# Second layer of a routed two-layer network: TensorE's order written out by pairs of slots, and up products that stream a high weight plane and its low partner in 512 columns

## The chip, the cores and the metric

The kernel runs on one core of a Trainium2 chip. A core has five engines, each with its own instruction stream, which meet at semaphores: TensorE (PE in the profile, its weight loads PEld), VectorE (DVE), ScalarE (ACT), GpSimd (POOL) and SyncE (SP), which only issues DMAs here. All time is device time in microseconds; the metric is the time of one execution. Three runs of the kernel before took 458.08, 459.53 and 459.67 us, a median of 459.53 us.

## The reference

The input goes through three parts. The first is an mLSTM over 768 steps for 2 x 8 heads of 40 columns. The second is a dense layer of 1536 tokens by 320 columns, with 2048 hidden columns and a softplus. The third is the second layer, and only it is touched by the change:

```
logits = x @ w_gate                       # 1536 tokens, 8 experts
e_idx  = argmax(logits)                   # one expert per token
gate_w = softmax(logits)[e_idx];  eom = sigmoid(x @ w_output_gate)
for e in range(8):                        # w1[e]: 320 x 1024, w2[e]: 1024 x 320
    h  = relu(x[e_idx == e] @ w1[e])
    out[e_idx == e] = gate_w * eom[:, e] * (h @ w2[e])
```

## The kernel before, in words

**Slots.** The tokens have been scattered into rows ordered by expert, and a slot is 128 such rows of one expert; NS = 15 slots are computed (four more that the code provides for have no work in the profiled execution). Each slot needs an up product (its 128 x 320 rows by the 320 x 1024 of w1), a relu, and a down product (128 x 1024 by the 1024 x 320 of w2), scaled per token by `cc`.

**Rounds.** The 1024 hidden columns are taken in NQ = 4 rounds (`qn`) of FQ = 256. In a round every slot has one up product into PSUM (`ph`), its relu, two transposes of 128 x 128 on TensorE (`tp`), and one down product of DM = 320 columns (`yp`), which is added to the slot's row of `yac`. The last round stores each `yac` row with an indirect DMA on POOL as soon as it is complete.

**Two-part operands.** Matmul operands are fp32r, so each fp32 number is split into a high part and a low part. `w1s` has five planes for each expert: three of high parts (rows 0 to 127, 128 to 255, and 256 to 319 with their low parts below them), then the low parts of the first two. `x2h` and `x2l` hold a slot's rows, turned, in high and low parts; `hh_` (printed as flat, as is `x2h`) and `hl_` (hl) the hidden columns. An up product is eight matmuls of 256 columns (`passes`, line 816), a down product six of 320. The weights are split anew in every round: a raw tile comes by DMA into a ring of seven buffers, ACT casts the high part (`split_w1`, line 1195; `split_w2`, line 1220), DVE subtracts for the low part (`low_w1`, line 1208; `low_w2`, line 1248), and POOL for the half plane of w1 (`low_w1p`, line 1214). Splits of w1 for the next round wait for this round's last up (`w1_read`), those of w2 for its last down (`w2_read`).

**What sets the order.** The instructions are emitted by a planner, the class `Weaver` (line 45). A task is a Python generator; each `yield` names the engines that its next step may run on ("A" ACT, "V" DVE, "G" POOL, "P" PE, "S" SP), a list of events to wait for, or takes a buffer from a `Ring`. The planner keeps a clock of each engine with prices of its own (`Priced`, line 149) and always emits the step that could start first; its rank decides a tie. Of several engines it takes the one that could start first, with a handicap of 10 us on DVE unless it is named first (`LAST`, line 42). Each engine then runs its instructions in the order emitted. In the second layer PE is asked for by several tasks: `slots` (line 1334) turns the rows of a slot, `up2` (line 1384) multiplies, `post` (line 1362) does relu, transposes and split, and `down2` (line 1417) begins a round's downs when its ups are done, in the last round as soon as it can. PSUM has eight banks: two for `ph`, three shared by the turned rows and `tp`, three for `yp`.

Nearly all instructions are emitted through one helper, so that the profile shows line 195 for them; the tile names tell them apart.

Of the kernel before, what the change touches and what calls it, by code (L numbers as in the profile page):

```python
# [23 lines left out]
P = 128  # L24
# [209 lines left out]
def mlstm_moe_kernel(ctx: ExitStack, tc: tile.TileContext, q_t, k_t, k, v, i_gate, f_gate, o_gate,  # L234
# [973 lines left out]
    def low_w1(qn, r, dst, ev):  # L1208
        yield "V"
        vsub(dst[:, 3:5], r[:, 0:2], dst[:, 0:2].bitcast(F32))  # L1210
        W.signal(ev)
        W.signal(w1_ready[qn])
# [35 lines left out]
    def low_w2(qn, e, r, ev):  # L1248
        yield "V"
        vsub(right["w2s"][:, 1, :, e, :], r, right["w2s"][:, 0, :, e, :].bitcast(F32))  # L1250
        W.signal(ev)
        W.signal(w2_ready[qn])
# [61 lines left out]
    ring = {t: Ring(ps2, t, n) for t, n in (("h", 2), ("t", 3), ("y", 3))}  # L1314
    ring["x"] = ring["t"]
# [12 lines left out]
    hr_ring = Ring(lp, "hr", 3)  # L1328
# [5 lines left out]
    def slots():  # L1334
        for s in range(NS):
            yield [slot_row[s]]
            row, row_ev = srow.pop(s)
            if s > 1:
                yield [begun[s - 2]]
            xp, ev = yield from ring["x"].get([P, 3, P], F32, "xslot")  # L1340
            yield "P"
            for kk in range(3):
                PE.transpose(xp[:, kk, :], row[:, kk * P:(kk + 1) * P], ident)
            W.signal(row_ev)
            W.add(after(W.cur.out, slot_x(s, xp, ev)), 0.1)
            W.add(after(slot_row[s], slot_c(s, row, row_ev)), 3)
# [15 lines left out]
    def post(qn, s, ph, hev):  # L1362
        hr, hr_ev = yield from hr_ring.get([P, FQ], F32, "hr")
        yield "AV"
        if W.cur.on == "A":
            ACT.activation(out=hr, in_=ph, func=AF.Relu)
        else:
            DVE.tensor_scalar(out=hr, in0=ph, scalar1=0.0, scalar2=None, op0=ALU.max)
        W.signal(hev)
        tp, ev = yield from ring["t"].get([P, 2, P], F32, "tp2")  # L1370
# [3 lines left out]
        W.signal(hr_ev)  # L1374
        if qn:
            yield [h_read[qn - 1, s]]
        yield "AV"
        copy(hh_[:, s], tp)
        yield "V"
        vsub(hl_[:, s], tp, hh_[:, s].bitcast(F32))  # L1380
# [3 lines left out]
    def up2():  # L1384
        for qn in range(NQ):
            yield [w1_ready[qn]]
            for s in range(NS):
                if qn == 0:
                    yield [slot_ready[s]]
                ph, hev = yield from ring["h"].get([P, FQ], F32, "ph2")  # L1390
                for n, (wt, xt, st, sp) in enumerate(passes(lambda a: w1v[:, a, bass.ds(evals[s] * FQ, FQ)], x2h[:, s], x2l[:, s])):
                    if n % 4 == 0:
                        yield "P"
                    PE.matmul(ph, xt, wt, start=st, stop=sp)
                if qn == 0:
                    W.signal(begun[s])
                W.add(after(W.cur.out, post(qn, s, ph, hev)), 1)
            W.signal(w1_read[qn])

    def reduce2(qn, s, yp, ev):  # L1400
        yield "V"
        if qn == 0:
# [14 lines left out]
    def down2():  # L1417
        for qn in range(NQ):
            yield [w2_ready[qn]] + ([w1_read[qn]] if qn < NQ - 1 else [])
            for s in range(NS):  # L1420
                yield [h_ready[qn, s]]
                yp, yev = yield from ring["y"].get([P, DM], F32, "yp")
                ew = bass.ds(evals[s] * DM, DM)
                order = [(j, xx, wi) for j in range(2) for xx, wi in ((hh_, 0), (hh_, 1), (hl_, 0))]
                for n, (j, xx, wi) in enumerate(order):
                    if n % 3 == 0:
                        yield "P"
# [132 lines left out]
```

## Time and profile before

| | |
|---|---|
| median of three runs | 459.53 us (458.08 to 459.67) |
| the profiled execution: its own time, its span | 458.13 us, 456.4 us |
| PE busy over the span | 421.3 us, 92% |
| DVE, ACT, POOL busy | 332.5, 309.3, 133.1 us (73%, 68%, 29%) |
| mean granted clock of TensorE | 0.965 of 2.4 GHz |
| from the first turned row of the second layer to its last PE product | 303.2 to 451.0 us |

The span runs from the first to the last instruction of the program; the execution's own time has 1.7 us around it. A matmul's recorded duration (some 0.3 us) is longer than the distance to the next one, since they are pipelined; the cost of one in a run of them is the distance between their starts.

In the rows below, a stage is printed as from:to and its length, then the busy time of PE, PEld, DVE, ACT and POOL with the number of instructions in brackets, then the granted clock of TensorE as a share of 2.4 GHz, the DMA engines' share and GB/s. A row of an engine in order of time has start, length, engine, line, operation, out<-in, the shapes and the count of instructions merged; a bracket behind it has the idle time before it and what ended it. A group has its count, its busy time, the mean of one in nanoseconds, and the idle time before its instructions with what ended it. `xslot` is the PSUM tile of turned rows.

### The profile page before, as it was taken

Reading aid. Unit: us, or ns where it says so; the run is one execution under the profiler, and the core shown is the slowest. Engines: PE = TensorE matmul, PEld = TensorE weight load, DVE = VectorE, ACT = ScalarE, POOL = GpSimd, SP = SyncE. Lnnn points to the kernel's source line nnn. Section 1 sums busy time; section 2 is a strip of 40 time slices with the busy share of each in tenths; the row PEclk is TensorE's granted clock in tenths of the full one; section 3 lists DMA queues with packets and bytes.
Section 4 is the critical chain, followed back from the end, with each engine's and each line's share of the span. In section 5 each row is a group of like instructions: output and inputs, shape, how many; then the busy total and the mean of one; then the engine's idle time right before and its main releaser. Section 6 shows DMA issues by size and latency. Waiting matters only on the chain.

```text
span 456.4 us, 10188 instructions
## 1 busy us (share of the span) xinstructions
PE 421.3 (92%) x3189; PEld 402.4 (88%) x3189; DVE 332.5 (73%) x866; ACT 309.3 (68%) x881; POOL 133.1 (29%) x222
## 2 busy tenths in 40 slices
PE   8669999999979999999999999768999999999694
PEld 7558999999879999999999998448899999999683
DVE  2998988769999998856666676565489499498332
ACT  1569799997769997887786786526656557638030
POOL 5256665545123410101010110231060060050633
PEclk9886999999999999999999999879999999999987
DMA  8969739396349423000010000175338348262211
GB/s 268 320 205 285 246 102 299 128 331 182 119 154 338 127 93 87 1 2 4 32 37 2 35 37 2 44 257 198 95 109 286 126 142 283 85 179 90 74 55 49
DMA packets 31772, 62.91 MB, mean 138 GB/s; under 512 B 3706, under 2 KB 16253, under 8 KB 31718
## 3 DMA queue, kind: packets, MB, share of 16 engines
q1 hardware_dynamic: 30230, 57.87, 39.8%
q0 software_dynamic: 1488, 4.35, 2.6%
q8 instruction: 30, 0.49, 0.4%
q14 instruction: 24, 0.20, 0.1%
HBM read 54.05 MB, written 8.65 MB: 137 GB/s over the span
## 4 chain that ended last, share of the span: by engine, by line
PE 71%; DVE 11%; ACT 11%; issue 4%; DMA 2%; SPq 1%; POOL 0%; POOLq 0%; DVEq 0%; ACTq 0%
PE ph L195 28%; PE acc L195 15%; PE yp L195 10%; ACT ab L195 4%; PE pv L195 4%; PE sp L195 4%; PE tp L195 3%; DVE wta L195 3%; DMA wra<-in_w_in_dram 2%; PE lg L195 2%; ACT w1s L195 1%; PE kv L195 1%; PE qc L195 1%; ACT gh L195 1%; ACT w2s L195 1%
## 5 line engine op out<-in xcount | busy, mean ns | idle before, releaser
L195 ACT ACTIVATE ab<-ab 128x256 f32<-128x256 f32 x192 | 78.2, 418 | 2.7
L195 DVE SCALAR_TENSOR_TENSOR g<-ph,ab 128x256 f32<-128x256 f32 x96 | 40.1, 419 | 24.4 <-ACT ab L195 23.7
L195 PE MATMUL ph<-w1s,flat 128*128 x300 | 56.6, 306 | 0.6 <-DVE w1s L195 0.6
L195 PE MATMUL acc<-win,gh 128*128 128x320 f32 x240 | 56.1, 318 | 0.5 <-ACT gh L195 0.5
L195 PE MATMUL yp<-w2s,flat 128*128 x240 | 54.2, 314 | 0.5 <-ACT flat L195 0.5
L195 POOL TENSOR_TENSOR w1s<-w1raw,w1s 64x256 fp32r<-64x256 f32 x32 | 29.7, 954 | 84.8 <-ACT w1s L195 83.0
L195 DVE TENSOR_TENSOR gl<-g,gh 128x256 fp32r<-128x256 f32 x96 | 46.4, 490 | 8.1 <-ACT gh L195 7.1
L195 ACT ACTIVATE ab<-ph 128x256 f32<-128x256 f32 x96 | 36.3, 379 | 18.1 <-PE ph L195 17.7
L195 ACT ACTIVATE hr<-ph 128x256 f32<-128x256 f32 x60 | 23.1, 385 | 34.2 <-PE ph L195 19.8
L195 PEld LDWEIGHTS ph<-w1s,flat 128*128 128x128 f32 x300 | 43.8, 190 | 1.3 <-DVE w1s L195 0.8
L195 PE MATMUL ph<-win 128*128 128x256 f32 x250 | 42.7, 291 | 0.0
L195 ACT CAST gh<-g 128x256 fp32r<-128x256 f32 x96 | 38.3, 401 | 5.8 <-DVE g L195 5.1
L195 DVE TENSOR_TENSOR hl<-tp,flat 128x256 fp32r<-128x256 f32 x60 | 25.1, 420 | 22.6 <-ACT flat L195 22.5
L195 PEld LDWEIGHTS yp<-w2s,flat 128*128 128x128 f32 x240 | 40.1, 190 | 0.7 <-ACT flat L195 0.7
L195 POOL DMA_INDIRECT rows<-row,rsm x12 | 12.2, 1020 | 94.6 <-ACT ab L195 30.7
L195 PEld LDWEIGHTS acc<-win,gh 128*128 128x128 f32 x240 | 38.6, 189 | 1.0 <-ACT gh L195 1.0
L195 PE MATMUL acc<-win,gl 128*128 128x320 f32 x120 | 37.4, 311 | 0.2 <-DVE gl L195 0.2
L195 PE MATMUL yp<-w2s,hl 128*128 x120 | 37.4, 312 | 0.0
L195 ACT CAST w2s<-w2raw 128x640 fp32r<-128x640 f32 x32 | 22.4, 726 | 21.3 <-PE yp L195 14.3
L195 PEld LDWEIGHTS ph<-win 128*128 128x128 f32 x250 | 35.6, 195 | 0.1
L195 PE MATMUL ph<-w1s,x2l 128*128 x180 | 33.9, 296 | 0.0
L195 PE MATMUL acc<-wou,gh 128*128 128x320 f32 x144 | 32.8, 313 | 0.3 <-ACT gh L195 0.3
(191 smaller groups left out, 1082.3 us busy)
## 6 DMA issues: line engine op xcount, KB each, us to landing
w1raw<-in_w_dram SPq DMA_DIRECT2D x32, 384.0 KB, 3.6
wra<-in_w_in_dram SPq DMA_DIRECT2D x16, 704.0 KB, 9.3
w2raw<-in_w_dram SPq DMA_DIRECT2D x32, 320.0 KB, 3.5
abc<-abc_dram SPq DMA_DIRECT2D x4, 1024.0 KB, 7.8
rows<-pad SPq DMA_DIRECT2D x19, 194.0 KB, 4.3
qT<-in_q_t_dram SPq DMA_DIRECT2D x6, 512.0 KB, 4.0
kn<-in_k_dram SPq DMA_DIRECT2D x5, 416.0 KB, 6.7
vn<-in_v_dram SPq DMA_DIRECT2D x6, 320.0 KB, 6.0
```

The source lines that it names most:

```text
L195: return fn(*args, **kw)
```

## The change

**Order of PE.** One task, `second`, replaces `slots`, `up2` and `down2`, and the transposes leave `post`: all PE work of the second layer is emitted in one written order, while ACT, DVE, POOL and SP are still planned. Four slots' rows are turned first. A round then goes by pairs of slots: two ups, the transposes of the pair before, and in the first round the rows of the pair two ahead. Behind the round's last up come two downs, the remaining transposes, and the other downs. In the last round downs begin behind the eighth up, up to three at a time.

**Up product.** `ph` grows from 256 to 512 columns, a whole bank. The first two matmuls stream a high plane of w1 and its low partner side by side (planes 0 and 3, then 1 and 4), 512 columns each; four more of 256 columns add to the first half: six matmuls in place of eight. ACT copies the second half out, DVE adds the first (`halves_sum`), and the relu moves behind the transposes (`split_h`).

**Rings and engines.** `ph` has three banks, `tp` two (a round's last slot takes one of `ph`), the turned rows share the three of `yp`; `hr` has four buffers. In rounds two to four the low parts of w1 and w2 may also run on POOL ("VG"), and in the first round the scaling of a down product may also run on ACT.

```diff
...
     def low_w1(qn, r, dst, ev):
-        yield "V"
-        vsub(dst[:, 3:5], r[:, 0:2], dst[:, 0:2].bitcast(F32))
+        yield "VG" if qn else "V"
+        (psub if W.cur.on == "G" else vsub)(dst[:, 3:5], r[:, 0:2], dst[:, 0:2].bitcast(F32))
         W.signal(ev)
         W.signal(w1_ready[qn])
 
...
     def low_w2(qn, e, r, ev):
-        yield "V"
-        vsub(right["w2s"][:, 1, :, e, :], r, right["w2s"][:, 0, :, e, :].bitcast(F32))
+        yield "VG" if qn else "V"
+        (psub if W.cur.on == "G" else vsub)(right["w2s"][:, 1, :, e, :], r, right["w2s"][:, 0, :, e, :].bitcast(F32))
         W.signal(ev)
         W.signal(w2_ready[qn])
 
...
     ps2 = tc.tile_pool(name="ps2", bufs=1, space=PSUM, reuse_waits="tile")
     ps2_cm, ps2 = ps2, ps2.__enter__()
-    ring = {t: Ring(ps2, t, n) for t, n in (("h", 2), ("t", 3), ("y", 3))}
-    ring["x"] = ring["t"]
+    ring = {t: Ring(ps2, t, n) for t, n in (("h", 3), ("t", 2), ("y", 3))}
+    ring["x"] = ring["y"]
 
...
-    hr_ring = Ring(lp, "hr", 3)
+    hr_ring = Ring(lp, "hr", 4)
 
-    def slots():
...
+    def turn_row(s):
+        yield [slot_row[s]]
+        row, row_ev = srow.pop(s)
+        xp, ev = yield from ring["x"].get([P, 3, P], F32, "xslot")
+        yield "P"
+        for kk in range(3):
+            PE.transpose(xp[:, kk, :], row[:, kk * P:(kk + 1) * P], ident)
+        W.signal(row_ev)
+        W.add(after(W.cur.out, slot_x(s, xp, ev)), 0.1)
+        W.add(after(slot_row[s], slot_c(s, row, row_ev)), 3)
 
     def slot_x(s, xp, ev):
         yield "AV"
...
-    def post(qn, s, ph, hev):
-        hr, hr_ev = yield from hr_ring.get([P, FQ], F32, "hr")
-        yield "AV"
-        if W.cur.on == "A":
-            ACT.activation(out=hr, in_=ph, func=AF.Relu)
-        else:
-            DVE.tensor_scalar(out=hr, in0=ph, scalar1=0.0, scalar2=None, op0=ALU.max)
+    hr_t, have_hr = {}, {(qn, s): Event() for qn in range(NQ) for s in range(NS)}
+
+    def halves_sum(qn, s, ph, hev):
+        hr_t[qn, s] = hr, _ = yield from hr_ring.get([P, FQ], F32, "hr")
+        yield "A"
+        ACT.copy(out=hr, in_=ph[:, 1])
+        yield "V"
+        DVE.tensor_tensor(out=hr, in0=ph[:, 0], in1=hr, op=ALU.add)
         W.signal(hev)
-        tp, ev = yield from ring["t"].get([P, 2, P], F32, "tp2")
+        W.signal(have_hr[qn, s])
+
+    def turn_h(qn, s):
+        yield [have_hr[qn, s]]
+        hr, hr_ev = hr_t.pop((qn, s))
+        tp, ev = yield from ring["h" if s == NS - 1 else "t"].get([P, 2, P], F32, "tp2")
         yield "P"
         for j in range(2):
             PE.transpose(tp[:, j, :], hr[:, j * P:(j + 1) * P], ident)
         W.signal(hr_ev)
+        W.add(after(W.cur.out, split_h(qn, s, tp, ev)), 1)
+
+    def split_h(qn, s, tp, ev):
         if qn:
             yield [h_read[qn - 1, s]]
         yield "AV"
-        copy(hh_[:, s], tp)
-        yield "V"
-        vsub(hl_[:, s], tp, hh_[:, s].bitcast(F32))
+        if W.cur.on == "A":
+            ACT.activation(out=hh_[:, s], in_=tp, func=AF.Relu)
+        else:
+            DVE.tensor_scalar(out=hh_[:, s], in0=tp, scalar1=0.0, scalar2=None, op0=ALU.max)
+        yield "V"
+        DVE.scalar_tensor_tensor(out=hl_[:, s], in0=tp, scalar=0.0, in1=hh_[:, s].bitcast(F32), op0=ALU.max,
+                                 op1=ALU.subtract)
         W.signal(ev)
         W.signal(h_ready[qn, s])
 
-    def up2():
+    def up(qn, s):
+        yield [slot_ready[s]]
+        ph, hev = yield from ring["h"].get([P, 2, FQ], F32, "ph2")
+        ew = bass.ds(evals[s] * FQ, FQ)
+        both = [(x2h[:, s, i], slice(i, i + 4, 3), slice(0, 2)) for i in range(2)]
+        one = [(xx[:, s, i], i, 0) for xx, i in ((x2h, 2), (x2l, 0), (x2l, 1), (x2l, 2))]
+        yield "P"
+        for n, (xt, a, to) in enumerate(both + one):
+            PE.matmul(ph[:, to], xt, w1v[:, a, ew], start=n == 0, stop=n == 5)
+        if qn == 0:
+            W.signal(begun[s])
+        W.add(after(W.cur.out, halves_sum(qn, s, ph, hev)), 1)
+
+    def down(qn, s):
+        yield [w2_ready[qn], h_ready[qn, s]]
+        yp, yev = yield from ring["y"].get([P, DM], F32, "yp")
+        ew = bass.ds(evals[s] * DM, DM)
+        order = [(j, xx, wi) for j in range(2) for xx, wi in ((hh_, 0), (hh_, 1), (hl_, 0))]
+        yield "P"
+        for n, (j, xx, wi) in enumerate(order):
+            PE.matmul(yp, xx[:, s, j, :], w2v[:, wi, j, ew], start=n == 0, stop=n == 5)
+        W.signal(h_read[qn, s])
+        W.add(after(W.cur.out, reduce2(qn, s, yp, yev)), 2)
+
+    def second():
+        for s in range(min(4, NS)):
+            yield from turn_row(s)
         for qn in range(NQ):
             yield [w1_ready[qn]]
-            for s in range(NS):
+            turned, downed = 0, 0
+            for s0 in range(0, NS, 2):
+                s1 = min(s0 + 2, NS)
+                for s in range(s0, s1):
+                    yield from up(qn, s)
+                if s1 == NS:
+                    W.signal(w1_read[qn])
+                if qn == NQ - 1 and s0 >= 6:
+                    for s in range(downed, min(s0 - 2, downed + 3)):
+                        yield from down(qn, s)
+                        downed = s + 1
+                elif s1 == NS:
+                    for s in range(2):
+                        yield from down(qn, s)
+                    downed = 2
+                for s in range(turned, s0):
+                    yield from turn_h(qn, s)
+                turned = s0
                 if qn == 0:
-                    yield [slot_ready[s]]
-                ph, hev = yield from ring["h"].get([P, FQ], F32, "ph2")
-                for n, (wt, xt, st, sp) in enumerate(passes(lambda a: w1v[:, a, bass.ds(evals[s] * FQ, FQ)], x2h[:, s], x2l[:, s])):
-                    if n % 4 == 0:
-                        yield "P"
-                    PE.matmul(ph, xt, wt, start=st, stop=sp)
-                if qn == 0:
-                    W.signal(begun[s])
-                W.add(after(W.cur.out, post(qn, s, ph, hev)), 1)
-            W.signal(w1_read[qn])
+                    for s in range(s0 + 4, min(s0 + 6, NS)):
+                        yield from turn_row(s)
+            for s in range(turned, NS):
+                yield from turn_h(qn, s)
+            for s in range(downed, NS):
+                yield from down(qn, s)
+            W.signal(w2_read[qn])
 
     def reduce2(qn, s, yp, ev):
-        yield "V"
-        if qn == 0:
+        yield "AV" if qn == 0 else "V"
+        if W.cur.on == "A":
+            ACT.activation(out=yac[:, s], in_=yp, func=AF.Copy, scale=cc[:, s:s + 1])
+        elif qn == 0:
             DVE.tensor_scalar(out=yac[:, s], in0=yp, scalar1=cc[:, s:s + 1], scalar2=None, op0=ALU.mult)
         else:
             DVE.scalar_tensor_tensor(out=yac[:, s], in0=yp, scalar=cc[:, s:s + 1], in1=yac[:, s],
...
-    def down2():
...
     W.add(load_rest(), 0)
     for qn in range(1, NQ):
         W.add(split_w2(qn), 4)
         W.add(split_w1(qn), 3)
-    W.add(up2(), 9.0)
-    W.add(down2(), 8)
+    W.add(second(), 0)
     W.run()
```

## Rows read from the trace of the kernel before

**Rows 1.** Busy time by stage in the second layer (from:to, length, then engines).
```profile
303.20:331.10 27.90, 26.04 (x193) 24.16 (x194) 13.74 (x29) 16.45 (x43) 3.52 (x28) 0.97 0.55 190
331.10:345.60 14.50, 13.96 (x96) 13.56 (x94) 13.30 (x25) 7.43 (x12) 6.90 (x8) 1.00 0.49 147
345.60:364.70 19.10, 19.07 (x148) 18.66 (x148) 11.87 (x22) 13.73 (x36) 0.00 (x0) 1.00 0.60 197
364.70:378.40 13.70, 13.62 (x94) 13.36 (x93) 12.66 (x24) 6.55 (x11) 7.52 (x8) 1.00 0.52 151
378.40:410.90 32.50, 32.41 (x243) 31.79 (x242) 24.95 (x47) 20.75 (x46) 7.52 (x8) 1.00 0.57 179
410.90:451.00 40.10, 34.26 (x241) 32.53 (x240) 20.63 (x39) 15.15 (x38) 13.80 (x14) 0.96 0.21 72
429.80:434.20 4.40, 0.04 (x1) 0.00 (x0) 0.55 (x1) 0.38 (x1) 3.00 (x4) 1.00 0.17 59
434.20:437.90 3.70, 3.61 (x16) 3.32 (x17) 0.85 (x2) 1.40 (x4) 0.00 (x0) 0.54 0.10 38
451.00:456.40 5.40, 0.00 (x0) 0.00 (x0) 0.55 (x1) 0.00 (x0) 0.98 (x1) 0.54 0.08 24
```

**Rows 2.** PE in order of time at the start of the third round.
```profile
378.42 0.75 PE L195 MATMUL ph<-w1s,flat 128*128 x5
...
379.36 0.76 PE L195 MATMUL ph<-w1s,flat 128*128 x5
...
380.51 0.86 PE L195 MATMUL ph<-w1s,flat 128*128 x5
...
381.60 0.38 PE L195 MATMUL tp<-ident,hr 128*128 128x128 f32 x2
381.74 0.84 PE L195 MATMUL ph<-w1s,flat 128*128 x5
```

**Rows 3.** The chain that ended last, three of its pieces (start, length, what).
```profile
398.25 12.77 PE yp L195 x87
...
429.84 4.37 issue
...
451.02 0.56 DVE yac L195
```

**Rows 4.** PE in order of time: the warm-up products ahead of the second layer.
```profile
300.45 2.72 PE L195 MATMUL warm<-ones 128*128 128x512 bf16 x6 [3.85 <-DVE w2s L195]
```

**Rows 5.** Busy time and granted clock of the stretch around those warm-up products.
```profile
300.40:303.20 2.80, 2.72 (x6) 0.69 (x5) 2.51 (x4) 0.00 (x0) 1.50 (x4) 0.50 0.86 249
```

**Rows 6.** PE in order of time in the first round, one pair of slots.
```profile
315.91 0.49 PE L195 MATMUL xslot<-ident,yac 128*128 128x128 f32 x3
316.24 0.38 PE L195 MATMUL tp<-ident,hr 128*128 128x128 f32 x2
...
317.66 0.41 PE L195 MATMUL tp<-ident,hr 128*128 128x128 f32 x2 [0.24 <-ACT hr L195]
```

**Rows 7.** DVE in order of time: the eighth sum of the last round.
```profile
432.27 0.55 DVE L195 SCALAR_TENSOR_TENSOR yac<-yp,cc,yac 128x320 f32<-128x320 f32 x1 [3.74 <-remote]
```

**Rows 8.** Groups of instructions by line and shape, 300 us to the end.
```profile
L195 DVE TENSOR_TENSOR hl<-tp,flat 128x256 fp32r<-128x256 f32 x60 | 25.1, 420 | 22.6 <-ACT flat L195 22.5
...
L195 DVE SCALAR_TENSOR_TENSOR yac<-yp,cc,yac 128x320 f32<-128x320 f32 x45 | 23.8, 544 | 10.8 <-PE yp L195 6.8 <-remote 3.7
L195 DVE TENSOR_TENSOR w2s<-w2raw,w2s 128x640 fp32r<-128x640 f32 x29 | 23.3, 820 | 3.7 <-ACT w2s L195 3.1
L195 ACT ACTIVATE hr<-ph 128x256 f32<-128x256 f32 x60 | 23.1, 385 | 34.2 <-PE ph L195 19.8 <-remote 12.0 <-PE tp L195 2.2
...
L195 POOL TENSOR_TENSOR w1s<-w1raw,w1s 64x256 fp32r<-64x256 f32 x24 | 21.9, 949 | 73.7 <-ACT w1s L195 73.7
L195 DVE TENSOR_TENSOR w1s<-w1raw,w1s 128x512 fp32r<-128x512 f32 x24 | 18.8, 782 | 1.9 <-ACT w1s L195 1.9
```

**Rows 9.** POOL in order of time: one of the stores of the result.
```profile
448.75 0.98 POOL L195 DMA_INDIRECT out_dram<-yac,tki  x1 [0.31 <-issue]
```

More of the change, by code (lines that the diff above doesn't have):

```diff
@@ L1332, in mlstm_moe_kernel @@
     h_read = {(qn, s): Event() for qn in range(NQ) for s in range(NS)}
-    def slots():
-        for s in range(NS):
[L1336 to L1340, printed above, removed]
-            yield "P"
[L1342 to L1346, printed above, removed]
+    def turn_row(s):
[8 more added lines that the diff above has]
+        W.add(after(slot_row[s], slot_c(s, row, row_ev)), 3)
     def slot_x(s, xp, ev):
@@ L1385, in up2 @@
+    def second():
+        for s in range(min(4, NS)):
+            yield from turn_row(s)
         for qn in range(NQ):
             yield [w1_ready[qn]]
-            for s in range(NS):
-                if qn == 0:
-                    yield [slot_ready[s]]
-                ph, hev = yield from ring["h"].get([P, FQ], F32, "ph2")
-                for n, (wt, xt, st, sp) in enumerate(passes(lambda a: w1v[:, a, bass.ds(evals[s] * FQ, FQ)], x2h[:, s], x2l[:, s])):
-                    if n % 4 == 0:
-                        yield "P"
-                    PE.matmul(ph, xt, wt, start=st, stop=sp)
-                if qn == 0:
-                    W.signal(begun[s])
-                W.add(after(W.cur.out, post(qn, s, ph, hev)), 1)
@@ L1415, in reduce2 @@
             tc.add_to_no_dep_group("result", r.ins)
-    def down2():
[L1418 to L1427, printed above, removed]
-                    PE.matmul(yp, xx[:, s, j, :], w2v[:, wi, j, ew], start=n == 0, stop=n == 5)
-                W.signal(h_read[qn, s])
-                W.add(after(W.cur.out, reduce2(qn, s, yp, yev)), 2)
-            W.signal(w2_read[qn])
-    W.add(slots(), 0)
     W.add(load_rest(), 0)
```

## The prediction

> **What bounds the kernel now.** I read the busy time by stage first, because the page's means cover layers that the change leaves alone. From 303.2 us on, the second layer runs as four rounds, one per quarter of the hidden columns: fifteen up products, then fifteen down products. In the first ups, the first downs, the second ups, the second downs and the third round PE is busy 26.04 of 27.9 us, 13.96 of 14.5, 19.07 of 19.1, 13.62 of 13.7 and 32.41 of 32.5 [rows 1]. There PE's own stream sets the end. DVE is close behind in the downs (13.30 of 14.5, 12.66 of 13.7). Only the last round is loose: PE 34.26 of 40.1 us, with 4.4 us in which it does almost nothing, 3.7 us at a mean granted clock of 0.54 behind them, and 5.4 us after its last product.
>
> The second view is PE's order of time, to see whether that stream can be shortened [rows 2]. Right behind a run of downs, one slot's eight up products of 256 columns take 0.94 us (378.42 to 379.36): 0.1175 us each. Two slots later, among the transposes, the eight take 1.09 us (380.51 to 381.60), and up plus transposes 1.23 us (380.51 to 381.74), with no idle named. So in the steady run ups cost about 0.136 us an instruction, more than their columns need.
>
> The third view is the chain that ended last: 87 down products in 12.77 us, 0.147 us each or 0.88 us a slot; the 4.37 us gap, named "issue"; DVE's last sum at 451.02 [rows 3].
>
> **The change part by part.** Nothing before 303.2 us changes, and the two kinds of split that may now run on POOL are those of rounds two to four.
>
> *Up products.* Eight instructions become six: two of 512 columns, four of 256; the columns stay 2048. The trace has no 512-column product of this type. 256 columns take 0.1175 us and 320 take 0.147, so 0.46 ns a column, which makes 512 columns 0.235: nothing gained. The other side is the 512-column bf16 warm-up, six in 2.72 us [rows 4] at a granted clock of 0.50 [rows 5], 0.453 each, 0.227 at full clock. One up then costs 2 x 0.227 to 0.235 + 4 x 0.1175 = 0.92 to 0.94. If 0.136 per instruction were the limit, six would need only 0.82, so the columns set it: I take 0.93, nearer to the rows of this type. The upper bound is that 1.09 stays.
>
> The Trainium skill (TensorE: Matmul & The Clock Gate, Back-to-back issue gap) gives a warm product its columns at full clock plus about 2.5 ns. By that, two joined products save 2.5 ns, 0.3 us over 120 of them, and widening as such is worth nothing. The row disagrees on the size (0.1175 us, where the rule gives 0.109 for 256 columns).
>
> *Turns.* A slot's two transposes lie between 1.23 - 0.94 = 0.29 and two of the 0.11 us below: I take 0.25. Three row transposes take 0.33 us (315.91 to 316.24) [rows 6]: 0.34 with their handover.
>
> *First round.* The transposes now wait: 0.24 us for ACT in the row shown [rows 6], and 27.9 - 26.04 = 1.9 us over the stage. In the written order a slot's rows are turned two pairs before its up, and its transposes come one pair behind, so these waits go. New ups: four rows turned first (12 x 0.11 = 1.3, and 0.6 allowed for rows that land late), 15 x 0.93 = 13.95, eleven more rows 3.74, twelve turns 3.0, and 1.0 allowed for handovers: 23.6 for 27.9, **-4.3 us**. New downs: 15 x 0.88 + 3 x 0.25 + 0.5 allowed at the boundary = 14.45 for 14.5, **0**.
>
> *Second and third round.* Ups 13.95 + 3.0 + 0.5 allowed = 17.45 for 19.1; downs 14.45 for 13.7. Together 31.9 for 32.8, **-0.9**, and for the third 31.9 for 32.5, **-0.6**.
>
> *Last round.* PE has 13.95 + 3.75 + 13.2 = 30.9 us of work. The first downs stand behind the eighth up, some 8.5 us into the round, while all eight w2 pieces are split by then only if ACT and DVE keep their pace: the round before interleaves them with the slots at about one a slot. I allow 2.0 us, between 0 and 4. What is queued behind that wait on PE is everything, but ACT and DVE catch up meanwhile. 32.9 for 40.1: **-7.2**. This takes the 4.4 us gap as gone. With the order of before it fell where two ups and a run of downs had been issued and DVE's eighth sum began only at 432.27, its releaser "remote" [rows 7]; no view shows what held it.
>
> *Added work off PE.* Each slot gets a copy of half a bank on ACT, in place of the relu there (0.385 us, the same shape [rows 8]), the relu moves into the copy behind the transposes, and DVE gets one sum of 256 more: sixty of about 0.42 us, the price of its low halves (hl), 6.3 us a round. In the second ups DVE has 11.87 us busy [rows 1]; 11.87 + 6.3 = 18.2 is more than the 17.45 expected. Starts of such rows overlap a little, and POOL may take some of the w2 low halves (0.82 each on DVE), so it is just hidden. What is late if not: the sum before a pair's transposes, and PE behind it. In the first round the yac products may go to ACT, which is busy only 7.43 of 14.5 us in the downs. In the other downs DVE keeps fifteen yac of 0.544 = 8.2 us, eight w1 low halves at 0.782 = 6.3 and a few sums; POOL takes the surplus. POOL's 64x256 piece takes 0.949 us, so 640 elements some 2.4 us and 512 some 1.9 (estimates in proportion; the lower bound is DVE's 0.82 and 0.78).
>
> Beside POOL, DVE's 512-element halves take 0.782 us, where 0.820 for 640 elements, made beside an idle POOL, would give 0.66: each is lengthened by 0.13. The Trainium skill (SBUF — State Buffer, Who interferes with whom) says that a DVE instruction with two SBUF inputs and a GpSimd one that reads SBUF block each other for the whole instruction, not in part. The trace shows less than that.
>
> *Tail.* The last down leaves one product, one DVE sum and one store as before. POOL's stores follow each other every 0.98 + 0.31 = 1.29 us [rows 9], the last three downs every 0.88: the last store starts about 1 us later. **+1.0**, between 0 and 2.
>
> **Sum.** -4.3 + 0 - 0.9 - 0.6 - 7.2 + 1.0 = -12.0 us. The profiled execution took 458.13 us for its span of 456.4, so 446.1; the median of the runs shown is 459.53, 1.4 above it, so about **447 us**. The allowances in it are 6.5 us: without them 441.
>
> **The rivals.**
> - *The gap stays* (0.18). Its cause is not shown, and stores and PE work overlap again. It costs 4.4 us and, at a clock of 0.54, some 1.7 of the 3.7 us behind it: 447.5 + 6 = 453.5. Against it: the order around it is new, and three earlier rounds with the same instructions have none.
> - *POOL's low halves come late* (0.12). Four w1 halves on POOL and its own eight pieces: 4 x 1.9 + 8 x 0.949 = 15.2 us against downs of 14. If DVE is also held for a whole POOL instruction, each of three boundaries waits about 2 us and the last round's first down 1.5 more: 447.5 + 7.5 = 455. For it: DVE's w1 halves stretched beside POOL. Against: there are only eight per round to share, and DVE may keep most.
> - *Ups stay at 1.09* (0.06): the extra is not per instruction, 60 x 0.16 = 9.6 us, 457.
> - *Slower: PE's fixed order waits for the sums* (0.14). A pair's transposes need ACT's copy (0.385), DVE's sum (0.42) and three handovers, some 1.3 us, of 2.6 us until PE arrives. If a w2 half (0.82) and two hl (0.84) stand in front on DVE, and a cast on ACT, it is about 0.7 us late, and a fixed order has nothing else to issue. In some 25 pairs (seven with row turns, eighteen beside w2 splits): 17.5 us, 465. It decides from 12.0 / 25 = 0.48 us a pair. For it: DVE's 18.2 us above. Against: each engine's sum is still at or under the phase, and the ring of up banks grows to three.
>
> **How the numbers follow.** Forecast 0.50, its own range 441 to 452. The others as given. 0.5% (2.3 us, 457.2 to 461.8) is about what a measurement can tell from no change. Faster by more: 0.50 + 0.18 + most of the 0.12 + half of the 0.06, 0.80. Within: 0.08. Slower: 0.12. The range 440 to 459 takes in all but the slower case.
>
> **What would show it.** Right: first ups near 24 us, a slot's up near 0.93 and up plus turn near 1.18, ACT and DVE with no PE wait behind them, the last round near 33 us without a gap, and a clock that stays at its upper level of 2.4 GHz until the last product. Wrong: a wait of PE's transposes for DVE's sum that returns in every pair; a wait at a boundary for POOL's w1s; a 512-column product well over 0.235 us apart.

## The result, and the profile after

On the chip of the first timing the changed kernel took 448.19 us (447.45 to 448.96, four runs) where the kernel before took 459.07 (458.08 to 459.67, four runs): a ratio of 0.9759 [0.9731, 0.9787]. The forecast was 447.

A second chip gave another picture. There the kernel before took 451.64 us (450.50 to 453.49, ten runs) and the changed one 447.08 (445.69 to 448.39, six runs): 0.9900 [0.9875, 0.9925]. The changed kernel differs by 1.1 us between them, the kernel before by 7.4. The last four experiments ran on a chip where the kernel before took 458.51; it is called the third here, but the record does not tell whether it is the first one again. So every ratio below is to the kernel before on the same chip. A few executions that took far longer than the others of their kernel, the profiled one of the experiment with late downs among them, are left out of every time and row.

The stages of the profiled execution on the first chip (447.45 us, span 445.8), cut where those of [rows 1] were: first ups, first downs, second ups, second downs, third ups, third downs, last round, tail.

```profile
304.00:326.70 22.70, 22.33 (x159) 20.55 (x160) 17.42 (x42) 15.10 (x42) 3.52 (x28) 0.99 0.68 238
326.70:341.00 14.30, 14.30 (x99) 13.93 (x98) 6.69 (x13) 13.16 (x26) 10.22 (x9) 1.00 0.58 171
341.00:358.40 17.40, 17.23 (x115) 15.32 (x115) 13.35 (x30) 13.51 (x35) 7.31 (x4) 1.00 0.59 194
358.40:372.90 14.50, 14.50 (x99) 13.95 (x97) 13.16 (x25) 7.26 (x12) 11.37 (x11) 1.00 0.50 152
372.90:390.70 17.80, 17.03 (x117) 15.54 (x116) 13.61 (x30) 13.19 (x34) 9.44 (x5) 1.00 0.61 204
390.70:405.20 14.50, 14.47 (x99) 13.94 (x97) 13.18 (x24) 7.26 (x12) 11.38 (x11) 1.00 0.51 159
405.20:438.50 33.30, 31.63 (x211) 29.24 (x210) 22.92 (x48) 14.89 (x38) 22.13 (x18) 1.00 0.21 72
438.50:445.80 7.30, 0.02 (x1) 0.00 (x0) 0.95 (x2) 0.00 (x0) 2.08 (x3) 0.68 0.15 53
```

TensorE is busy nearly the whole of every ups and downs stage, and its granted clock is 0.99 of 2.4 GHz in the first ups and 1.00 from there to the last product. The last round has no hole: 33.3 us where it had 40.1. The tail grew from 5.4 to 7.3. The kernel before, profiled on the second chip, has these first ups and this last round:

```profile
303.00:331.10 28.10, 26.08 (x194) 24.16 (x194) 14.12 (x30) 16.58 (x43) 4.20 (x30) 0.96 0.56 196
...
410.60:444.10 33.50, 32.47 (x242) 31.24 (x240) 20.80 (x39) 15.11 (x38) 13.80 (x14) 1.00 0.25 87
```

Its first ups are as slow as on the first chip, but its last round takes 33.5 us: there is no gap to remove. Its chain of waits passes the place of the gap [rows 3] with nothing between products and transposes:

```profile
421.24 7.04 PE yp L195 x48
428.28 1.41 PE ph L195 x12
429.69 0.22 PE tp L195 x2
```

All stages in us, from the same views (the second chip's changed kernel was cut likewise):

| stage | predicted | after, chip 1 | before, chip 2 | after, chip 2 |
|---|---|---|---|---|
| first ups | 23.6 | 22.7 | 28.1 | 22.8 |
| first downs | 14.45 | 14.3 | 13.6 | 14.3 |
| second round | 31.9 | 31.9 | 33.5 | 32.0 |
| third round | 31.9 | 32.3 | 32.4 | 32.3 |
| last round | 32.9 | 33.3 | 33.5 | 33.3 |
| tail | 6.4 | 7.3 | 5.4 | 7.1 |
| sum | 141.15 | 141.8 | 146.5 | 141.8 |

The steady run of the third ups, which answers to [rows 2]:

```profile
378.05 0.83 PE L195 MATMUL ph<-w1s,flat 128*128 x3
378.72 0.52 PE L195 MATMUL ph<-w1s,x2l 128*128 x3
379.07 0.74 PE L195 MATMUL ph<-w1s,flat 128*128 x3
...
380.01 0.60 PE L195 MATMUL tp<-ident,hr 128*128 128x128 f32 x4
380.37 0.82 PE L195 MATMUL ph<-w1s,flat 128*128 x3
```

A pair of slots, two ups and four transposes, goes from 378.05 to 380.37: 2.32 us, 1.16 a slot where it was 1.23. The up right behind transposes takes 1.02 us, the second one 0.94, the four transposes 0.36. All waits of TensorE in the second layer (engine, tile and line, what it waited for, us in total, times, longest):

```profile
PE ph L195 <- DVE hr L195: 1.5, 2, 0.8
PE yp L195 <- POOL w2s L195: 0.8, 1, 0.8
PE xslot L195 <- DMA yac<-rows: 0.2, 1, 0.2
```

The two for DVE's sum fall at the starts of the third and the last round (376.65 and 408.90), where the fourth up needs the bank that the first slot's sum frees; the one for POOL's low half at the last round's first down (415.72). The groups of the second layer that answer to [rows 8]:

```profile
L195 POOL TENSOR_TENSOR w2s<-w2raw,w2s 128x640 fp32r<-128x640 f32 x14 | 26.2, 1892 | 8.9 <-issue 4.9 <-ACT w2s L195 4.0
L195 DVE TENSOR_TENSOR hr<-ph,hr 128x256 f32<-128x256 f32 x60 | 24.6, 421 | 18.6 <-ACT hr L195 15.7 <-issue 2.7
L195 DVE TENSOR_TENSOR w1s<-w1raw,w1s 128x512 fp32r<-128x512 f32 x17 | 15.0, 881 | 4.8 <-ACT w1s L195 4.8
L195 DVE TENSOR_TENSOR w2s<-w2raw,w2s 128x640 fp32r<-128x640 f32 x12 | 14.5, 1207 | 1.9 <-ACT w2s L195 1.9
L195 POOL TENSOR_TENSOR w1s<-w1raw,w1s 128x512 fp32r<-128x512 f32 x7 | 9.7, 1385 | 34.8 <-ACT w1s L195 34.5
```

POOL took 14 low halves of w2 at 1.89 us and 7 of w1 at 1.39. DVE's own low half of w2 beside them rose from 0.82 to a mean of 1.21.

### The profile page after: what moved, and what is told of

Same layout as the page of the kernel before. It is cut to its first block, busy times and chain, and to the rows that moved or that the text cites. A ratio compares the mean times of both kernels' runs of the same rounds, so it can differ in the third digit from the quotient of the medians.

```text
span 445.8 us, 9825 instructions
## 1 busy us (share of the span) xinstructions
PE 415.6 (93%) x3069; PEld 393.1 (88%) x3069; DVE 335.0 (75%) x890; ACT 313.7 (70%) x896; POOL 170.0 (38%) x243
## 4 chain that ended last, share of the span: by engine, by line
PE 71%; ACT 10%; DVE 10%; issue 3%; DMA 3%; POOL 2%; SPq 1%; POOLq 0%; DVEq 0%; ACTq 0%
PE ph L195 25%; PE acc L195 15%; PE yp L195 11%; PE pv L195 5%; ACT ab L195 4%; PE sp L195 4%; PE tp L195 2%; DVE wta L195 2%; DVE w2s L195 2%; DMA wra<-in_w_in_dram 2%; PE kv L195 2%; PE qc L195 2%; PE lg L195 2%; ACT w2s L195 2%; ACT w1s L195 1%
## 5 line engine op out<-in xcount | busy, mean ns | idle before, releaser
L195 DVE SCALAR_TENSOR_TENSOR g<-ph,ab 128x256 f32<-128x256 f32 x96 | 40.1, 419 | 24.9 <-ACT ab L195 24.1
L195 POOL TENSOR_TENSOR w1s<-w1raw,w1s 64x256 fp32r<-64x256 f32 (+1 forms) x39 | 40.8, 1061 | 47.0 <-ACT w1s L195 44.4
L195 ACT ACTIVATE ab<-ph 128x256 f32<-128x256 f32 x96 | 36.3, 378 | 17.8 <-PE ph L195 17.4
L195 PE MATMUL ph<-w1s,flat 128*128 x180 | 47.2, 370 | 1.5 <-DVE hr L195 1.5
L195 DVE TENSOR_TENSOR hr<-ph,hr 128x256 f32<-128x256 f32 x60 | 24.6, 421 | 18.6 <-ACT hr L195 15.7
L195 ACT COPY hr<-ph 128x256 f32<-128x256 f32 x60 | 22.6, 377 | 20.3 <-PE ph L195 19.7
L195 PEld LDWEIGHTS ph<-w1s,flat 128*128 128x128 f32 x180 | 29.7, 189 | 4.5 <-DVE hr L195 1.9
L195 PE MATMUL ph<-w1s,x2l 128*128 x180 | 31.1, 281 | 0.0
```

The source lines that it names most:

```text
L195: return fn(*args, **kw)
```

## The experiments

The first eight ran on the second chip, the last four on the third. The expectations of the first four (eight products to late downs) count from the first chip's 459.1 and 448.2 us, those of the last four from the second chip's 451.6 and 447.1, so it is the differences that can be held against the results.

**Eight products in the written order.**

```
-        both = [(x2h[:, s, i], slice(i, i + 4, 3), slice(0, 2)) for i in range(2)]
+        both = [(x2h[:, s, i], i + 3, 1) for i in range(2)] + [(x2h[:, s, i], i, 0) for i in range(2)]
...
-            PE.matmul(ph[:, to], xt, w1v[:, a, ew], start=n == 0, stop=n == 5)
+            PE.matmul(ph[:, to], xt, w1v[:, a, ew], start=n in (0, 2), stop=n in (1, 7))
```

> The changed kernel with each 512-column up product taken apart again into two of 256: eight instructions a slot, the same columns, the same written order of TensorE, the same copy on ScalarE and sum on VectorE. Theory of the prediction (columns alone set an up's price): a slot still 0.93 us, the time unchanged at 448.2 (within 0.9). Rival (an up product whose address comes from a register also costs a fixed step of some 0.136 us an instruction, as in the steady run before, and the downs and transposes give only part of it back): an up of 1.0 to 1.09 us where ups follow each other, 45 to 60 slots by 0.05 to 0.15, so 450.5 to 457.

449.16 us, ratio 0.9938 [0.9910, 0.9965], against 0.9900 [0.9875, 0.9925] for the changed kernel: about 2 us slower by the medians, between the two expectations, though the two intervals overlap a little. TensorE at the start of its second ups shows both of them in turn:

```profile
341.13 0.75 PE L195 MATMUL ph<-w1s,flat 128*128 x5
...
342.07 0.82 PE L195 MATMUL ph<-w1s,flat 128*128 x5
...
343.15 0.82 PE L195 MATMUL ph<-w1s,flat 128*128 x5
...
344.24 0.82 PE L195 MATMUL ph<-w1s,flat 128*128 x5
...
345.33 0.60 PE L195 MATMUL tp<-ident,hr 128*128 128x128 f32 x4
```

The first up takes 0.94 us, the next three 1.08 to 1.09: 0.136 an instruction, the pace of the steady run before [rows 2]. With six products the four ups in this place take 0.93 to 0.95 each (340.97 to 344.73 on the first chip). Later, with four transposes behind every pair, pairs of eight go at 2.34 us (354.73, 357.07, 359.41), all but the 2.32 of the changed kernel. So there is a cost per instruction: it shows where ups follow each other, and in the kernel before with two transposes behind each up, but hardly with four behind each pair. One wait of 0.96 us for DVE (351.59) is in these 2 us too.

**The written order alone.**

```
-        ph, hev = yield from ring["h"].get([P, 2, FQ], F32, "ph2")
+        ph, hev = yield from ring["h"].get([P, FQ], F32, "ph2")
...
-            PE.matmul(ph[:, to], xt, w1v[:, a, ew], start=n == 0, stop=n == 5)
+            PE.matmul(ph, xt, wt, start=st, stop=sp)
...
-        yield "A"
-        ACT.copy(out=hr, in_=ph[:, 1])
-        yield "V"
-        DVE.tensor_tensor(out=hr, in0=ph[:, 0], in1=hr, op=ALU.add)
+        yield "AV"
...
```

> The changed kernel with the up product of before: eight products of 256 columns into half a bank, one relu in place of copy and sum, plain copy and subtraction behind the transposes. What is left of the change is the written order, the rings, and the choice of engines. Theory: the order carries the first round (-4) and the last (-7), so 448 to 451 us; VectorE is relieved of 60 sums of 0.42 us, so the two waits for a sum at 376.65 and 408.90 (0.77 and 0.74) go. Rival (the six-instruction up is what shortened the rounds, about 60 x 0.15): 455 to 458.

446.83 us, 0.9899 [0.9879, 0.9919]: the same as the whole change. The waits for DVE's sums are gone; steady pairs take 2.33 us (377.87 to 380.19 to 382.53). The rival falls.

**The wide product alone.** The same edit the other way round, in the kernel before: six products into a whole bank, copy, sum, relu behind the transposes.

```
-                ph, hev = yield from ring["h"].get([P, FQ], F32, "ph2")
+                ph, hev = yield from ring["h"].get([P, 2, FQ], F32, "ph2")
...
-                    PE.matmul(ph, xt, wt, start=st, stop=sp)
+                    PE.matmul(ph[:, to], xt, w1v[:, a, ew], start=n == 0, stop=n == 5)
```

> The kernel before with only the up product changed: two products of 512 and four of 256 columns, copy on ScalarE, sum on VectorE, relu behind the transposes; its planned order, its rings, its engines stay. Theory: the wide product as such takes 0.15 us off an up only in the steady run, and the sum makes the way from up to transposes longer by some 0.5 us, with two ph banks only: 456 to 461. Rival (instructions are what costs): 60 x 0.15 less, 450 to 452. The 4.4 us gap in the last round stays under the first, since nothing of its order changes.

453.02 us, 1.0051 [1.0032, 1.0069]: slower by 2.3 us by the ratio (1.4 by the medians). TensorE's transposes wait nine times for DVE's sum, 4.2 us in all; in the kernel before on this chip they wait six times for ACT's relu, 1.7 us in all. In the order that the planner finds, the wide product costs more than it saves; in the written order it comes out even. Order alone, wide alone and both give -4.6, +2.3 and -4.5 us by their ratios: on this chip all of the gain is the written order's, with its rings and engines.

**Late downs in the kernel before.**

```
-            yield [w2_ready[qn]] + ([w1_read[qn]] if qn < NQ - 1 else [])
+            yield [w2_ready[qn]] + [w1_read[qn]]
```

> The kernel before with one condition changed: in the last round, too, the downs wait for the last up, as in the three rounds before. Ups 17 to 18 us from 410.9, downs 13.7; the first store can start near 430.5 and fifteen stores by 1.29 us end the last one's start at 448.5, about 5 us to the end: 455 if the 4.4 us gap goes with the overlap of downs and ups. If the gap belongs to the stores or to something else that stays: 458 to 461.

456.60 us, 1.0120 [1.0095, 1.0145]: about 5 us slower. This chip has no gap, so the run could not tell what was asked. It prices something else: downs among the last round's ups are worth about 5 us here. That this is because the stores then begin early is argued from the order, not read from a trace.

**The kernel before and the changed kernel, unchanged.**

> The kernel before, unchanged, profiled beside the others, because its runs took 451.6 us beside the first four experiments where they took 459.1 beside the changed kernel. Theory: what differs is the last round of the second layer alone: the first turned row again within 0.5 us of 303.2, the rounds of the same lengths, but the 4.4 us in which TensorE does nothing, and the stretch at a mean granted clock of 0.54 behind it, gone or short, and the time about 451.6. Rival: the time is shorter everywhere by about 1.6 per cent, the second layer then begins near 298 us and the gap stays.

> The changed kernel, unchanged, beside the kernel before on the same chip. If the gap of the kernel before is what comes and goes between chips, the changed kernel, which has none, keeps its 448.2 us (447.4 to 449.0) while the kernel before takes 451 to 452: a ratio of 0.992. Rival: both kernels are faster on this chip by the same 1.6 per cent, 441 us, a ratio of 0.976.

451.21 us for the one, a single run; 447.08 us, 0.3 under its range, and 0.9900 for the other. The first theory holds in both: the second layer begins at 303.0 us, and only the gap is missing, as the rows above show.

**Low halves on DVE alone.**

```
-        yield "VG" if qn else "V"
+        yield "V"
...
-        yield "VG" if qn else "V"
+        yield "V"
```

> The changed kernel with the low halves of w1 and w2 on VectorE alone, as before the change. VectorE gets back 21 halves (14 of w2 by 0.82, 7 of w1 by 0.78: 17 us in three rounds) and loses what GpSimd's work adds to its own (17 halves of w2 by 0.27 and 17 of w1 by 0.10: 6 us). Theory: the waits of TensorE at round starts (0.77, 0.74 and 0.83 us) come from halves stretched beside GpSimd, so 1 to 2 us less, 446 to 447.5. Rival: VectorE is the tight engine in the ups (18.2 us of work for 17.5), the sums come later, 450 to 454.

445.38 us, 0.9865 [0.9840, 0.9890]. The median stands 1.7 us under the changed kernel's, but the two intervals overlap (0.9875 to 0.9890), so it is likely, not certain, that this beats the changed kernel. DVE's low halves return to the price of before:

```profile
L195 DVE TENSOR_TENSOR w2s<-w2raw,w2s 128x640 fp32r<-128x640 f32 x25 | 20.0, 812 | 4.0 <-ACT w2s L195 4.0
L195 DVE TENSOR_TENSOR w1s<-w1raw,w1s 128x512 fp32r<-128x512 f32 x24 | 18.4, 768 | 4.2 <-ACT w1s L195 4.2
```

The waits of TensorE move rather than go: 1.5 us for DVE's last w2 half in the last round, 1.3 for its w1 halves, 2.8 together where the changed kernel on this chip has 2.4. The second and the third ups are shorter (first up to first down 16.7 and 17.0 us, where the changed kernel on this chip has 17.5 and 17.8), though 0.68 us of the waits for w1 stands right ahead of the third.

**The same with the written order alone.** The edit just shown, in the kernel of the second experiment.

> The written order with eight products of 256 columns and the plain relu (the 446.8 us kernel of the first four), and the low halves on VectorE alone. Without the sixty sums VectorE has room for all the halves, so if GpSimd's share is only a loss, 445 to 446.5; if it is what keeps the halves in time, 448 to 450.

445.21 us, 0.9850 [0.9825, 0.9875]: as the one before it. POOL's share is a small loss whether or not DVE has the sums to do.

**Transposes right behind their own pair.**

```
-                for s in range(turned, s0):
+                for s in range(turned, s1):
                     yield from turn_h(qn, s)
-                turned = s0
+                turned = s1
```

> The changed kernel with each pair's hidden columns turned right behind the pair's own ups, not one pair later. This prices the slower rival of the prediction (TensorE's fixed order waits for the sums): a copy of 0.377, a sum of 0.421 and handovers of some 0.5 us stand between the pair's last up and its transposes, with nothing else to issue but, in the first round, nothing at all. 28 pairs (four rounds by seven) by 1.0 to 1.4 us: 447.1 + 28 to 39 = 475 to 486. Rival (TensorE's queue and the rings hide part of it): below 460.

475.37 us, 1.0367 [1.0337, 1.0397]: the prediction's slower rival, made real. (The changed kernel was not timed on this chip; at the first chip's ratio it would take 0.9759 x 458.51 = 447.5, so 28 us less.) From the second ups, and TensorE's longest wait over the second layer:

```profile
361.16 0.83 PE L195 MATMUL ph<-w1s,flat 128*128 x3
...
363.27 0.44 PE L195 MATMUL tp<-ident,hr 128*128 128x128 f32 x2
364.21 0.44 PE L195 MATMUL tp<-ident,hr 128*128 128x128 f32 x2 [0.51 <-DVE hr L195]
364.41 0.83 PE L195 MATMUL ph<-w1s,flat 128*128 x3
```

```profile
PE tp L195 <- DVE hr L195: 18.7, 24, 1.9
```

A pair takes 3.25 us (361.16 to 364.41) in place of 2.32, and 28 pairs by 0.93 make 26 us. The waits named for the sum make 18.7 us in 24 places; the rest of the 28 is not named. One pair of distance hides all of that.

**Rows turned one pair ahead.**

```
-        for s in range(min(4, NS)):
+        for s in range(min(2, NS)):
             yield from turn_row(s)
...
-                    for s in range(s0 + 4, min(s0 + 6, NS)):
+                    for s in range(s0 + 2, min(s0 + 4, NS)):
                         yield from turn_row(s)
```

> The changed kernel with rows turned one pair ahead of their up in place of two (two turned first, each pair's rows behind the pair before). Theory (the first round's gain comes from rows turned early enough that VectorE's low half of them, x2l, is done): a cast and a low half of 384 columns for each of two rows stand before the next ups, some 2.2 us against the 0.5 us of transposes in between, so seven pairs wait 1 to 2 us: 454 to 461, and the first ups again near 30 us. Rival (the pairs alone give it): 447 to 449.

451.17 us, 0.9838 [0.9819, 0.9858], 3.7 us over those 447.5, where 7 to 14 were expected. The first ups, cut as before, and the longest wait of TensorE:

```profile
302.40:329.80 27.40, 24.65 (x159) 21.07 (x160) 17.69 (x42) 14.98 (x42) 3.54 (x28) 0.99 0.52 183
```

```profile
PE ph L195 <- ACT flat L195: 2.7, 8, 0.6
```

27.4 us where the changed kernel has 22.7 and the kernel before 27.9: with the rows near, nearly the whole gain of the first round is lost. It is less than expected: the ups wait at most 0.6 us each time, for ACT's cast and not for DVE's low half. These waits make 2.7 of the 4.7 us; the rest is not named.

**Rows turned farther ahead in the kernel before.**

```
-    ring["x"] = ring["t"]
+    ring["x"] = ring["y"]
...
-            if s > 1:
-                yield [begun[s - 2]]
+            if s > 3:
+                yield [begun[s - 4]]
```

> The kernel before with one part of the change: a slot's rows are turned up to four slots ahead of its up (two before), in the three banks of the down products, so that the hidden columns keep their three. Its planned order is otherwise kept. Theory (the early rows are the first round's gain): first ups 28.0 to 24.5, and 448 to 449. Rival (the order by pairs is needed, since transposes of the hidden columns wait for the relu there): 451 to 452.

455.72 us, 0.9936 [0.9916, 0.9956], 2.8 us faster, where 2.6 to 3.6 were expected. The first ups take 24.8 us (303.5 to 328.3) in place of 27.9: this edit gives about 3 of the 5 us. It also moves the turned rows to other banks, and the two were not separated. The rest is left to the order by pairs.

**Downs one pair later.** In the kernel with low halves on DVE alone:

```
-                if qn == NQ - 1 and s0 >= 6:
+                if qn == NQ - 1 and s0 >= 8:
```

> The changed kernel with the low halves on VectorE alone (445.4 us in the four before) and the last round's downs one pair later, behind the tenth up. TensorE there waited 1.5 us for VectorE's last low half of w2 at the first down; with a pair's 2.3 us of other work in front that wait goes, and the fifteen stores (1.29 us each) begin some 1 us later and end 0.5 to 1 us later behind the last sum: 444 to 445. Rival (the stores' queue sets the end, since it has less time left): 445.5 to 447.

448.32 us, 0.9770 [0.9750, 0.9791]. The wait for w2 is gone, but TensorE lost 3.27 us to "issue" before the last three downs: the gap, in a new place. Being on another chip, it can't be set against 445.38.

**What the gaps have in common.** The third chip has the gap, as the first had. The kernel before on the first chip, TensorE and then ACT; and the same copy of ACT on the second chip:

```profile
428.74 0.75 PE L195 MATMUL ph<-w1s,flat 128*128 x5
...
434.21 0.54 PE L195 MATMUL tp<-ident,hr 128*128 128x128 f32 x2 [4.37 <-issue]
```

```profile
433.77 0.38 ACT L195 ACTIVATE hr<-ph 128x256 f32<-128x256 f32 x1 [11.98 <-remote]
```

```profile
428.85 0.39 ACT L195 ACTIVATE hr<-ph 128x256 f32<-128x256 f32 x1 [7.20 <-PE ph L195]
```

The experiment with rows farther ahead keeps the kernel before's last round; TensorE, ACT, then POOL's stores there (the first and the last of the row):

```profile
426.41 0.52 PE L195 MATMUL ph<-w1s,x2l 128*128 x3
431.41 0.69 PE L195 MATMUL tp<-ident,hr 128*128 128x128 f32 x2 [4.48 <-issue]
```

```profile
430.97 0.38 ACT L195 ACTIVATE hr<-ph 128x256 f32<-128x256 f32 x1 [12.08 <-remote]
```

```profile
420.77 1.02 POOL L195 DMA_INDIRECT out_dram<-yac,tki  x1 [17.57 <-DVE yac L195]
...
430.28 0.98 POOL L195 DMA_INDIRECT out_dram<-yac,tki  x1 [0.75 <-DVE yac L195]
```

And the experiment with downs one pair later, TensorE, ACT and POOL:

```profile
433.96 0.82 PE L195 MATMUL tp<-ident,hr 128*128 128x128 f32 x6
438.05 0.90 PE L195 MATMUL yp<-w2s,flat 128*128 x2 [3.27 <-issue]
```

```profile
437.61 0.66 ACT L195 ACTIVATE flat<-tp 128x256 fp32r<-128x256 f32 x2 [5.71 <-remote]
```

```profile
430.28 0.98 POOL L195 DMA_INDIRECT out_dram<-yac,tki  x1 [1.64 <-DVE yac L195]
...
436.92 0.98 POOL L195 DMA_INDIRECT out_dram<-yac,tki  x1 [0.49 <-issue]
```

The profile says "issue" for TensorE, but in all three TensorE starts again 0.06 us after ACT's first instruction there ends (433.77 + 0.38 = 434.15, then 434.21; 431.35, then 431.41; two of ACT are merged in the third row, one takes 0.38, so 437.99, then 438.05), and what it then does needs what ACT has just made. So TensorE waits for ACT, whose instruction starts late. In the kernel before, the relu of an up starts 0.26 us after the next up has begun on the second chip (428.59, then 428.85), and 5.03 us after it on the first (428.74, then 433.77). Its releaser there is "remote", as for DVE's eighth sum [rows 7]: the signal came when no recorded instruction had just ended. Since the ends of matmuls are modelled, the rows do not tell whether the product or only its signal was late.

In all three a row of stores runs meanwhile. TensorE comes back 0.13 to 0.15 us after the end of the row's last store (434.08, 431.26 and 437.90), but that store had itself waited for a late sum, so this order of times shows no cause. The first DVE sum that is late behind a finished product comes 4.30, 4.38 and 4.33 us after the row's first store (427.99 in the kernel before, where the row begins at 423.69, then 425.15 and 434.61), so within the fourth store of a row without a pause. Rows of three show a little of it too: in the changed kernel on the first chip two of ACT's copies come 1.28 and 1.58 us behind the copy before them (421.18 and 426.42, as the third store of a row ends), on the second chip 0.94. TensorE has a pair's work in front there and loses nothing.

On the second chip, the kernel before issues eleven stores in such a row (423.53 to 436.45) and no sum is late. So in these traces the lateness goes with a row of stores, and with the chip. The changed order gives rows of two or three, because two or three downs are followed by ups and transposes; only its last five stores form a longer row, with short pauses. There the kernel with rows one pair ahead, on the third chip, loses 0.51 us before 439.02. This was read from the traces afterwards: a kernel with its stores spaced on purpose was not run, so that the stores cause it is not shown, and what makes ACT and DVE late on those chips is open.

## Why the prediction was right, point by point

- *Up products.* Right where ups follow each other: an up takes 0.93 to 0.95, and a 512-column product starts about 0.23 us before the next (three of 512, 512 and 256 columns in 0.58, 341.92 to 342.50). Columns set it, as taken. The Trainium skill (TensorE: Matmul & The Clock Gate, Back-to-back issue gap) gives a warm product by itself its columns and only about 2.5 ns more, so that widening is worth next to nothing. Behind a run of downs the runs agree, since two products of 256 columns take 0.235 us and one of 512 takes 0.23; where eight products cost 0.136 each they do not. What the prediction left out is that six instructions keep the column pace there and eight do not. That pays for the sum that the wide product needs, and no more.
- *Turns.* Two sizes were off and cancel. The up behind transposes takes 1.02, not 0.93, and four transposes take 0.36, where 2 x 0.25 was taken: a pair takes 2.32 for 2.36. That the ups stages came out so close is luck to this extent.
- *First round.* Right in cause: two experiments, one each way, tie the gain to rows turned early. Size -5.2 in place of -4.3, since the 1.0 us allowed for handovers was not needed: a pair with its rows takes 2.98 (311.84 to 314.82), where the terms without it make 3.04. The four rows ahead took 2.3 (304.03 to 306.34) for 1.9.
- *Second and third round.* 31.9 and 32.3 for 31.9. The third's 0.4 lies within its wait of 0.77 us for a sum that stood behind a stretched w2 half (376.65).
- *Last round.* 33.3 for 32.9. The w2 wait was 0.83 for 2.0, the 0.74 for a sum at its start was not counted, and the work took 31.7 for 30.9. The term of -7.2 is right on the first chip and was rightly read as the gap. It is not slack in the order, though: on the second chip the same edit gives -0.2, because there the kernel before has no gap. The prediction took a gap without a known cause as gone, and that it was there to be removed was luck of the chip: on the second one the whole change gives -4.6 us, not -12.0.
- *Tail.* +1.9 for +1.0, near the upper bound of 2. On the second chip, +1.7 (7.1 for 5.4): the last store starts 1.7 us behind the last product's end (436.9, then 438.62), where it was 0.8, so the +1.0 was sized well; the rest lies behind that start, 5.4 us to the end where it was 4.6, which the prediction did not have and no row explains. On the first chip the last two sums come late as well. DVE in the changed kernel there, and on the second chip:

```profile
436.80 0.55 DVE L195 SCALAR_TENSOR_TENSOR yac<-yp,cc,yac 128x320 f32<-128x320 f32 x1 [0.29 <-PE yp L195]
438.35 0.55 DVE L195 SCALAR_TENSOR_TENSOR yac<-yp,cc,yac 128x320 f32<-128x320 f32 x1 [1.00 <-PE yp L195]
439.82 0.55 DVE L195 SCALAR_TENSOR_TENSOR yac<-yp,cc,yac 128x320 f32<-128x320 f32 x1 [0.93 <-PE yp L195]
```

```profile
436.09 0.55 DVE L195 SCALAR_TENSOR_TENSOR yac<-yp,cc,yac 128x320 f32<-128x320 f32 x1 [0.33 <-PE yp L195]
436.97 0.55 DVE L195 SCALAR_TENSOR_TENSOR yac<-yp,cc,yac 128x320 f32<-128x320 f32 x1 [0.33 <-PE yp L195]
```

  The sums follow the products every 0.88 us on the second chip; counted from the first one shown, the last two on the first chip are 0.67 and 1.26 late.
- *The rivals.* The gap did not stay, but what the rival said of it (stores and PE work overlap) is what the gaps have in common. POOL's low halves cost some 2.3 us in three places, not 7.5: 0.83 for a half of its own, 0.77 and 0.74 for sums behind a w2 half of DVE that took 1.73 beside POOL. Ups did not stay at 1.09. The slower rival did not come: sums were late at two round starts, not in every pair; with the transposes one pair earlier it came with 28 us.
- *The stretch of DVE beside POOL.* Under-sized. The prediction read 0.13 us from [rows 8] against the Trainium skill's rule of a block for the whole instruction (SBUF — State Buffer, Who interferes with whom). With POOL on 640-element halves DVE's own rose by 0.39 in the mean, up to 0.91 (1.73 at 406.78). That is nearer to the rule, though short of POOL's 1.89.

Predicted 141.15 us for these stages, measured 141.8; the second layer also began 0.8 us later (304.0). Together 1.4 us, the distance from the forecast's 446.1 to the 447.45 of the profiled execution. The allowances that the prediction puts at 6.5 us add up to 6.1; its 441 without them stands.

## What to carry to other kernels

An engine that runs in a fixed order needs the inputs that other engines make for it one full group of work ahead: here one pair hides a copy, a sum and their handovers, and without it the kernel is 28 us slower. Read the pace of an instruction both behind a run of others and in the middle of one; where the two differ (0.94 and 1.09), fewer and wider instructions can help only in the second place. And when a gap has no named cause, time the kernel before on another chip before crediting a change with its removal.

## What the runs showed of the hardware

- On the first and the third chip ACT and DVE started late behind TensorE's products, by up to some 4.9 us (430.97 for 426.1 in the experiment with rows farther ahead), while POOL's indirect stores followed each other every 1.29 us; it showed from the third or fourth store of a row on, and TensorE then stood 3.3 to 4.5 us, named "issue", for what ACT had not yet made. On the second chip eleven stores in a row did nothing of the kind, and there the program was the same as on the first. That the stores cause it was not tested.
- Eight up products of 256 columns follow each other every 0.1175 us or every 0.136, by what stands before them. What sets the 0.136 was not tested.
- POOL's subtraction of 640 elements by 128 rows took 1.89 us and of 512 elements 1.39, less than the 2.4 and 1.9 that were worked out from its 64x256 piece.
